# Giving the stores of the first layer's sums a later due time in a list-scheduled two-layer kernel

## The chip, the cores and the metric

One core of one Trainium2 chip runs the whole program. The metric is the device time of one execution in microseconds (us), taken as the median of several runs.

## The reference

The input is 8192 tokens of 192 values. A seven-tap convolution with softmax weights comes first, then two feed-forward layers with 2048 hidden units, each `x @ w_in`, an elementwise function, `@ w_out`:

```
x = attn_out.reshape(B * S, D)
h = np.maximum(x @ w_in, 0.0);  x = h * h @ w_out        # layer 0
h = x @ w_in;                   out = h * np.cos(h) @ w_out   # layer 1
```

All of it is float32. The kernel keeps that precision by writing each factor as a high part (`hi`, rounded) and a low part (`lo`, the rest), and by multiplying the parts on TensorE.

## The kernel before, in words

**Tiles.** The tokens are cut into 16 blocks of 512. For each layer m and block b there are 16 tiles f, one per 128 hidden units. So 512 tiles are counted through by t. Their order is `phases`: the first six blocks of layer 0, then layer 1 and layer 0 in turn, (1,0), (0,6), (1,1), (0,7) and so on, and the last six blocks of layer 1. For b from 5 on, block (0,b) ends at tile 96 + 32(b - 5) - 1, and 16 tiles of layer 1 follow it. A *site* below is such a stretch of 16 layer-1 tiles; there are eleven, for b = 5 to 15.

**What one tile does.** TensorE multiplies x by `w_in` into a PSUM bank `h` (line 618). For layer 1, `between` (from line 705) then scales and rounds on ACT (`rr`, line 721), subtracts on DVE (line 724), takes the absolute value and the sine on ACT (lines 726 and 727), multiplies by h on DVE (line 729, which is the last reader of the bank), and splits the product: `hi` is a copy (line 277 on ACT, line 279, a CAST, on DVE) and `lo` the difference (line 284, DVE or POOL). Six tiles later (`LAG`) TensorE multiplies `hi` and `lo` by `w_out` into the banks `acc` (line 642). There are four `h` banks, six `hi`, five `lo` and one set of `acc`.

**What follows a block.** Seven tiles after block (0,b) has ended, `take_x2(b)` adds up its sums and makes the second layer's input of them: four copies and additions out of `acc` (lines 277 and 740), then the *split*: a move between halves (`x2u`, line 277), its addition (`x2s`, line 748), two high parts on ACT (`x2t`, line 277) and two differences on DVE or POOL (`x2t` and `x2s`, line 284). Four stores on SP's queue (lines 770, 772, 775) write it to DRAM as `x2d`, from where `fetch` reads it as `X(1, b)` up to ten blocks later. `x2t` lies in the buffer `xt`, `x2s` in `sum`; there is one of each, and `take_out`, which does the same for layer 1, uses both next.

**Who sets the order.** The kernel lists all operations first and a scheduler (`Order.issue`) then puts them into engine queues. Each operation names the engines that it may run on, with a cost. A backward pass gives each operation a due time: TensorE's work is due at its place in time, a store at its `by`, and everything else early enough for its users. The forward pass takes, among the operations that could begin at once, the one with the earliest due time, and picks the engine on which it would end first. `clock(t)` is the planned time of tile t; a tile counts 2.155 us (`PACE`). Once built, each engine's queue is fixed and runs in order.

Of the kernel before, what the change touches and what calls it, by code (L numbers as in the profile page):

```python
# [25 lines left out]
LEAD = 6  # L26
# [34 lines left out]
class Order:  # L61
# [12 lines left out]
    def buf(self, pool, shape, dtype, tag, n, name):  # L74
        old = self.tags.setdefault(tag, [])
        b = Buf(
            lambda: pool.tile(shape, dtype, tag=tag, bufs=n, name=name),
            old[-n] if len(old) >= n else None, old[-1] if old else None,
        )
        old.append(b)  # L80
        return b
# [14 lines left out]
    def op(self, ways, fn, reads=(), writes=(), size=0, behind=None, by=1e9, over=(), since=0.0,  # L96
           alone=True, slack=0.0, ahead=0.0, drag=0.0):
        o = Op()
        o.ways, o.fn, o.size, o.drag = ways, fn, size, drag
        o.alone, o.slack, o.ahead = alone, slack, max(ahead, self.ahead)  # L100
        o.late = self.SENT + size / self.RATE + self.SEEN if size else 0.0
        o.behind, o.by, o.since = behind, by, max(since, self.since)
        o.older, o.deps, o.after, o.n = set(over), set(), set(behind or ()), len(self.ops)
        for write, accesses in ((False, reads), (True, writes)):
            for a in accesses:
                b, key = a if isinstance(a, tuple) else (a, None)
                for p, w, k in b.log:
                    if (w or write) and (k is None or key is None or k == key):
                        o.deps.add(p)
                if b.log:  # L110
                    o.after.add(b.log[0][0])
                elif b.before is not None:
                    o.after.add(b.before.log[0][0])
                if b.older is not None:
                    o.older.add(b.older)
                b.log.append((o, write, key))
        o.deps.discard(o)
        o.after.discard(o)
        self.ops.append(o)
        return o  # L120
# [57 lines left out]
def act(n, psum=False):  # L178
    return (0.05 if psum else 0.093) + n / 1200


def dve(n, fast=False, psum=False):
    return 0.147 + n / 960 if psum else 0.069 + n / (1600 if fast else 900)


def pool(n, scalar=False):
    return 0.1 + n * 0.0011 if scalar else 0.13 + n * 0.0023
# [3 lines left out]
def conv_moe_kernel(  # L191
# [40 lines left out]
    def sbuf(shape, dtype, tag, n, name):  # L232
        return buf(sb, shape, dtype, tag, n, name)
# [41 lines left out]
    def copy(e, out, in_):  # L275
        if e == "act":
            nc.scalar.activation(out, in_, AF.Copy)  # L277
        elif e == "dve":
            nc.vector.tensor_copy(out, in_)  # L279
        else:  # L280
            nc.gpsimd.tensor_scalar(out=out, in0=in_, scalar1=1.0, scalar2=0.0, op0=ALU.mult, op1=ALU.add)

    def sub(e, out, in0, in1):
        eng[e].tensor_tensor(out=out, in0=in0, in1=in1, op=ALU.subtract)  # L284
# [316 lines left out]
    def clock(t):  # L601
        return START + (early / NF * t if t < NF else early + PACE * (t - NF))

    first, final = {}, {}
# [134 lines left out]
    def sums(o, v0, w0, a1, u):  # L739
        add = lambda out, in0, in1: nc.vector.tensor_tensor(out=out, in0=in0, in1=in1, op=ALU.add)  # L740
        (low0, low1), (high0, high1) = o[0], o[-1]
        op({"act": act(N, True), "dve": dve(N, psum=True)}, lambda e: copy(e, v0(), high0.t), [high0], w0, alone=False)
        op({"act": act(N, True), "dve": dve(N, psum=True)}, lambda e: copy(e, a1.t, high1.t), [high1], [a1], alone=False)
        if len(o) > 1:
            op({"dve": dve(N, psum=True)}, lambda e: add(v0(), low0.t, v0()), [low0], w0, alone=False)
            op({"dve": dve(N, psum=True)}, lambda e: add(a1.t, low1.t, a1.t), [low1], [a1], alone=False)
        op({"act": act(N)}, lambda e: copy(e, u.t, a1.t[DB:P]), [a1], [u])
        op({"dve": dve(N), "pool": pool(N)}, lambda e: eng[e].tensor_tensor(
            out=a1.t[0:DB], in0=a1.t[0:DB], in1=u.t, op=ALU.add), [u], [a1])


    def take_x2(b):
        o = acc.pop((0, b))
        xt = sbuf([P, 2, BS * D], F32R, "xt", 1, f"x2t{b}")
        s = sbuf([P, N], F32, "sum", 1, f"x2s{b}")
        u = sbuf([DB, N], F32, "raw", 2, f"x2u{b}")
        there = src[b] = buf(dram, [2, D, N], F32, f"x2_{b}", 1, f"x2d{b}")
        v = lambda: xt.t[:, 1, 0:N].bitcast(F32)
        sums(o, v, [(xt, 1)], s, u)
        op({"act": act(N)}, lambda e: copy(e, xt.t[:, 0, 0:N], v()), [(xt, 1)], [(xt, 0)])  # L760
        op({"dve": dve(N), "pool": pool(N)}, lambda e: sub(e, xt.t[:, 1, 0:N], v(), xt.t[:, 0, 0:N].bitcast(F32)),
           [(xt, 0)], [(xt, 1)])
        rest = lambda: xt.t[0:DB, :, N:BS * D]
        wide = lambda: s.t[0:DB].rearrange("d (w n) -> d w n", w=2)
        op({"act": act(N)}, lambda e: copy(e, rest(), wide()), [s], [(xt, 2)])
        op({"dve": dve(N), "pool": pool(N)}, lambda e: sub(
            e, wide().bitcast(F32R), wide(), rest().bitcast(F32)), [(xt, 2)], [s])
        due = clock(final[0, b] + 12)
        for w in range(2):
            op({"sp": 0.5}, lambda e, w=w: nc.sync.dma_start(out=there.t[w, 0:P], in_=xt.t[:, w, 0:N].bitcast(F32)),  # L770
               [(xt, w)], [(there, w)], size=P * N * 4, by=due)
        op({"sp": 0.5}, lambda e: nc.sync.dma_start(
            out=there.t[0, P:D].rearrange("d (w n) -> d w n", w=2), in_=rest().bitcast(F32)), [(xt, 2)], [(there, 2)],
           size=DB * N * 4, by=due)
        op({"sp": 0.5}, lambda e: nc.sync.dma_start(out=there.t[1, P:D], in_=s.t[0:DB]),
           [s], [(there, 3)], size=DB * N * 4, by=due)
# [29 lines left out]
    for b in range(NB):  # L806
        when(final[0, b] + LAG + 1, take_x2, b)
        when(final[1, b] + LAG + 1, take_out, b)
        t = first[1, b]
        when(t - 8, x2, b)  # L810
        if b == 0:
            continue
        t = first[0, b]
        ago = lambda n: max(t - n, -1)
        far = NF + (4 if b < LEAD else 12)
        if b > 1:
            when(ago(far + 8), load_x, b)
        if b % CB == 0:
            c = b // CB
            if c == 1:  # L820
                when(ago(2 * NF - 6), load_g, c)
                when(ago(2 * NF - 9), soon, softmax, c, 0, CB)
            else:
                n = 14 + 9 * c
                when(n, early_exp, c, clock(n) + 15)
                when(max(ago(NF + far), n + 2), late_softmax, c)
        if b == 1:
            for i in range(BS):
                when(i, second_slot, i)
            when(4, second_x1)  # L830
            continue
        for n, f in ((far, attend), (far - 8, x1)):
            when(ago(n), *([soon] if b == CB else []), f, b)
# [69 lines left out]
```

## Time and profile before

| what | value |
|---|---|
| median of 3 runs | 1185.49 us (1185.39 to 1186.48) |
| the profiled execution | 1183.92 us |
| its span | 1182.1 us, 1.8 us less |
| busy: TensorE, ACT, DVE, POOL | 97%, 87%, 81%, 47% |

Busy shares are means over the whole span. TensorE's matmuls overlap, so idle time shows better in the row of its weight loads (PEld), which carry the waits.

### The profile page before, as it was taken

The numbers are of one execution on the slowest core, as the hardware profiler recorded it, in microseconds if no ns is written. First come the engines' busy times: TensorE is split into PE (matmuls) and PEld (weight loads), VectorE is DVE, ScalarE is ACT, GpSimd is POOL, SyncE is SP. The second block draws the span as 40 slices with busy tenths as digits, with TensorE's granted clock in tenths as the row PEclk, the third lists the DMA queues.
The fourth block names the chain that finished last, engine by engine and source line by source line (L and its number), as shares of the span: only waits on it lengthen the run. The fifth ranks groups of instructions, "written<-read, shape, count | busy, mean of one in ns | idle before, by whom it ended". The sixth has DMA issues, their size and how long they took to land.

```text
span 1182.1 us, 25854 instructions
## 1 busy us (share of the span) xinstructions
PE 1152.2 (97%) x9922; PEld 949.9 (80%) x9922; DVE 955.4 (81%) x1381; ACT 1023.7 (87%) x1892; POOL 550.8 (47%) x427
## 2 busy tenths in 40 slices
PE   7998999999999999999999999999999999999997
PEld 7776888887888888788887878888888888888885
DVE  7788788788897968879698887978757657888886
ACT  2897999999888897988889898888988889999996
POOL 0227557886363555525455452642603315544442
PEclk8999999999999999999999999999999999999999
DMA  8606877652443533344352344334143323223301
GB/s 207 185 18 158 242 183 201 164 141 70 94 115 68 123 81 66 91 95 122 64 118 62 62 115 81 78 71 95 35 87 82 68 55 81 40 42 68 68 9 20
DMA packets 126540, 112.96 MB, mean 96 GB/s; under 512 B 58192, under 2 KB 95568, under 8 KB 126416
## 3 DMA queue, kind: packets, MB, share of 16 engines
q1 hardware_dynamic: 124928, 110.78, 39.9%
q8 instruction: 78, 1.28, 0.5%
q10 hardware_dynamic: 1488, 0.52, 0.3%
q14 instruction: 46, 0.38, 0.1%
HBM read 78.70 MB, written 31.26 MB: 93 GB/s over the span
## 4 chain that ended last, share of the span: by engine, by line
PE 72%; ACT 11%; DVE 8%; DMA 4%; issue 2%; SPq 2%; POOL 1%; DVEq 0%; ACTq 0%
PE acc L642 37%; PE h L618 34%; ACT rr L721 2%; DVE lo L284 2%; ACT hi L277 2%; ACT rr L726 2%; DVE rr L729 2%; ACT rr L727 2%; DVE rr L724 2%; PE second L508 1%; SPq L501 1%; DVE hi L279 1%; ACT x2t L277 1%; DMA xc<-in_x_dram 1%; DMA X(0, 10)_136<-x1d 1%
## 5 line engine op out<-in xcount | busy, mean ns | idle before, releaser
L642 PE MATMUL acc<-hi,wo 64*128 64x512 f32 x3054 | 958.3, 387 | 1.4 <-DVE x2t L740 1.2
L642 PE MATMUL acc<-lo,wo 64*128 64x512 f32 x2036 | 774.8, 388 | 1.2 <-DVE lo L284 1.1
L642 PEld LDWEIGHTS acc<-hi,wo 64*128 64x128 f32 x3054 | 543.3, 184 | 59.6 <-DVE x2t L740 2.0
L284 POOL TENSOR_TENSOR lo<-rr,hi 128x512 fp32r<-128x512 f32 x187 | 244.9, 1313 | 410.2 <-DVE hi L279 163.2
L642 PEld LDWEIGHTS acc<-lo,wo 64*128 64x128 f32 x2036 | 374.7, 184 | 41.4 <-DVE lo L284 4.5
L284 DVE TENSOR_TENSOR lo<-rr,hi 128x512 fp32r<-128x512 f32 x229 | 205.3, 909 | 71.3 <-ACT hi L277 34.2
L456 POOL TENSOR_TENSOR pr<-xc,wgen_late 128x672 f32<-128x672 f32 x96 | 168.0, 1830 | 98.6 <-DVE at L471 79.1
L724 DVE SCALAR_TENSOR_TENSOR rr<-rr,h 128x512 f32<-128x512 int32 x256 | 173.8, 683 | 44.5 <-ACT rr L721 42.5
L711 ACT ACTIVATE rr<-h 128x512 f32<-128x512 f32 x256 | 152.5, 597 | 59.8 <-PE h L618 58.8
L729 DVE TENSOR_TENSOR rr<-h,rr 128x512 f32<-128x512 f32 x256 | 173.1, 685 | 29.5 <-ACT rr L727 28.2
L277 ACT ACTIVATE hi<-rr 128x512 fp32r<-128x512 f32 x288 | 178.8, 627 | 14.9 <-DVE rr L729 12.8
L726 ACT ACTIVATE rr<-rr 128x512 f32<-128x512 f32 x256 | 156.8, 626 | 27.2 <-DVE rr L724 27.1
L727 ACT ACTIVATE rr<-rr 128x512 f32<-128x512 f32 x256 | 157.9, 626 | 1.5
L721 ACT ACTIVATE rr<-h 128x512 int32<-128x512 f32 x256 | 149.8, 587 | 4.8 <-PE h L618 3.8
L715 ACT ACTIVATE rr<-rr 128x512 f32<-128x512 f32 x158 | 99.3, 629 | 2.1
L471 DVE TENSOR_REDUCE at<-pr 128x192 f32<-128x1344 f32 x56 | 86.2, 1545 | 0.4
L284 DVE TENSOR_TENSOR lo<-h,hi 128x512 fp32r<-128x512 f32 x96 | 64.1, 686 | 20.3 <-PE acc L642 15.1
L279 DVE CAST hi<-rr 128x512 fp32r<-128x512 f32 x128 | 64.6, 505 | 8.6 <-DVE rr L729 0.5
L277 ACT ACTIVATE hi<-h 128x512 fp32r<-128x512 f32 x96 | 57.9, 605 | 4.0 <-PE acc L642 2.7
L715 ACT ACTIVATE h<-rr 128x512 f32<-128x512 f32 x94 | 57.3, 612 | 1.6
L336 POOL TENSOR_TENSOR wilo_early<-wilo_early,wihi_early 128x384 uint32<-128x384 uint32 x16 | 17.0, 1070 | 59.2 <-DVE wilo_early L334 53.1
L618 PE MATMUL h<-X(0, 2)_110,wihi 64*128 64x512 f32 x96 | 28.6, 388 | 1.1 <-DMA X(0, 2)_110<-x1d 1.1
(237 smaller groups left out, 2910.3 us busy)
## 6 DMA issues: line engine op xcount, KB each, us to landing
xc<-in_x_dram SPq DMA_DIRECT2D x14, 960.0 KB, 6.0
x1d<-xt SPq DMA_DIRECT2D x104, 96.0 KB, 2.1
x2d<-x2t SPq DMA_DIRECT2D x32, 256.0 KB, 2.5
out_dram<-out SPq DMA_DIRECT2D x64, 64.0 KB, 2.0
rawo<-in_moe_w_out_dram SPq DMA_DIRECT2D x8, 384.0 KB, 3.6
x2d<-x2t SPq DMA_DIRECT2D x16, 128.0 KB, 2.6
x2d<-x2s SPq DMA_DIRECT2D x16, 128.0 KB, 2.4
out_dram<-ob SPq DMA_DIRECT2D x30, 64.0 KB, 1.9
```

The costliest lines, as they stand in the source:

```text
L277: nc.scalar.activation(out, in_, AF.Copy)
L284: eng[e].tensor_tensor(out=out, in0=in0, in1=in1, op=ALU.subtract)
L456: eng[e].tensor_tensor(out=t.rearrange("p k (h g) -> p k h g", h=H)[:, :, hs], in0=xc[b].t[:, i:i + K, :].rearrange("p k (h g) -> p k h g" ...
L618: return lambda: nc.tensor.matmul(h.t, lhsT=w[m].t[q, s, c], rhs=x[q, v, s], start=n == 0, stop=n == len(ops) - 1)
L642: nc.tensor.matmul(o[a].t, lhsT=wo[m].t[q, f, W[w]], rhs=p[v].t[q], start=f == 0 and n in (0, 3), stop=f == last_f and n in (2, 4))
L711: op({"act": act(N, True)}, lambda e: nc.scalar.activation(r.t, h.t, AF.Relu), [h], [r])
L715: nc.scalar.activation(g.t, r.t, AF.Square)
L721: op({"act": act(N, True)}, lambda e: nc.scalar.activation(k(), h.t, AF.Identity, scale=INV_2PI), [h], [r])
L724: op({"dve": dve(N, psum=True)}, lambda e: nc.vector.scalar_tensor_tensor(out=r.t, in0=k(), scalar=-TWO_PI, in1=h.t, op0=ALU.mult, op1=ALU ...
L726: op({"act": act(N)}, lambda e: nc.scalar.activation(r.t, r.t, AF.Abs), [], [r])
L727: op({"act": act(N)}, lambda e: nc.scalar.activation(r.t, r.t, AF.Sin, scale=-1.0, bias=math.pi / 2), [], [r], behind=exps if (b, f) == (0 ...
L729: op({"dve": dve(N, psum=True)}, lambda e: nc.vector.tensor_tensor(out=r.t, in0=h.t, in1=r.t, op=ALU.mult), [h], [r], alone=False)
```

## The change

The four stores of `take_x2` are due 18 tiles behind the end of their block instead of 12, for b >= 5 (`LEAD` is 6). That is 6 x 2.155 = 12.9 us later on the scheduler's clock, and by the backward pass the split in front of them is due later as well. No operation is added or taken out.

```diff
-        due = clock(final[0, b] + 12)
+        due = clock(final[0, b] + (18 if b >= LEAD - 1 else 12))
         for w in range(2):
             op({"sp": 0.5}, lambda e, w=w: nc.sync.dma_start(out=there.t[w, 0:P], in_=xt.t[:, w, 0:N].bitcast(F32)),
                [(xt, w)], [(there, w)], size=P * N * 4, by=due)
```

TensorE's queue stays the same row for row. The other queues are the same up to tile 96. From there, ACT has 18 rows more, DVE 11 and POOL 9 rows fewer (neighbouring equal rows are one), because the scheduler also chooses other engines: CASTs of `hi` on DVE go from 128 to 100, and ACT takes the 28. On SP only the order among the four stores of a block changes. The differences stand in the sites, and in the last 80 tiles.

ACT behind block (0,6), where `x2u6`, `x2t6` and `x2s6` belong to the split and the other names carry their tile. Before:

```order
L277 ACTIVATE x2u6_4881<-x2s6_4836 64x512
L721 ACTIVATE rr134_4900<-h134_4852 128x512
L277 ACTIVATE x2t6_4813<-x2t6_4813 128x512
L726 ACTIVATE rr133_4861<-rr133_4861 128x512
L726 ACTIVATE rr134_4900<-rr134_4900 128x512
L727 ACTIVATE rr133_4861<-rr133_4861 128x512
L277 ACTIVATE x2t6_4813<-x2s6_4836 64x2x256
L727 ACTIVATE rr134_4900<-rr134_4900 128x512
L721 ACTIVATE rr135_4944<-h135_4889 128x512
L277 ACTIVATE hi133_4950<-rr133_4861 128x512
```

and with the change:

```order
L277 ACTIVATE x2u6_4881<-x2s6_4836 64x512
L721 ACTIVATE rr134_4900<-h134_4852 128x512
L277 ACTIVATE hi132_4902<-rr132_4832 128x512
L726 ACTIVATE rr133_4861<-rr133_4861 128x512
L726 ACTIVATE rr134_4900<-rr134_4900 128x512
L727 ACTIVATE rr133_4861<-rr133_4861 128x512
L727 ACTIVATE rr134_4900<-rr134_4900 128x512
L721 ACTIVATE rr135_4935<-h135_4889 128x512
L277 ACTIVATE x2t6_4813<-x2t6_4813 128x512
L277 ACTIVATE hi133_4947<-rr133_4861 128x512
```

The first `x2t6` copy has moved behind six rows, the second has left this stretch, and `hi132` has come to ACT.

DVE at the same place. Before:

```order
L724 SCALAR_TENSOR_TENSOR rr134_4900<-rr134_4900,h134_4852 128x512
L279 CAST hi132_4925<-rr132_4832 128x512
L729 TENSOR_TENSOR rr133_4861<-h133_4822,rr133_4861 128x512
L729 TENSOR_TENSOR rr134_4900<-h134_4852,rr134_4900 128x512
L724 SCALAR_TENSOR_TENSOR rr135_4944<-rr135_4944,h135_4889 128x512
L284 TENSOR_TENSOR lo132_4967<-rr132_4832,hi132_4925 128x512
L284 TENSOR_TENSOR lo133_4979<-rr133_4861,hi133_4950 128x512
L729 TENSOR_TENSOR rr135_4944<-h135_4889,rr135_4944 128x512
```

and with the change:

```order
L724 SCALAR_TENSOR_TENSOR rr134_4900<-rr134_4900,h134_4852 128x512
L284 TENSOR_TENSOR lo132_4925<-rr132_4832,hi132_4902 128x512
L729 TENSOR_TENSOR rr133_4861<-h133_4822,rr133_4861 128x512
L729 TENSOR_TENSOR rr134_4900<-h134_4852,rr134_4900 128x512
L724 SCALAR_TENSOR_TENSOR rr135_4935<-rr135_4935,h135_4889 128x512
L724 SCALAR_TENSOR_TENSOR rr136_4963<-rr136_4963,h136_4917 128x512
L729 TENSOR_TENSOR rr135_4935<-h135_4889,rr135_4935 128x512
```

The CAST of `hi132` is gone, `lo132` stands in its place, and `lo133` has left the queue.

POOL at the same place. Before:

```order
L748 TENSOR_TENSOR x2s6_4836<-x2s6_4836,x2u6_4881 64x512
L284 TENSOR_TENSOR x2t6_4813<-x2t6_4813 128x512
L284 TENSOR_TENSOR x2s6_4836<-x2s6_4836,x2t6_4813 64x512
L284 TENSOR_TENSOR lo134_4992<-rr134_4900,hi134_4965 128x512
L284 TENSOR_TENSOR lo135_5012<-rr135_4944,hi135_5003 128x512
```

and with the change:

```order
L748 TENSOR_TENSOR x2s6_4836<-x2s6_4836,x2u6_4881 64x512
L284 TENSOR_TENSOR x2t6_4813<-x2t6_4813 128x512
L284 TENSOR_TENSOR lo133_4975<-rr133_4861,hi133_4947 128x512
L284 TENSOR_TENSOR lo134_4990<-rr134_4900,hi134_4977 128x512
L284 TENSOR_TENSOR lo135_5025<-rr135_4935,hi135_5008 128x512
L284 TENSOR_TENSOR lo136_5050<-rr136_4963,hi136_5039 128x512
L284 TENSOR_TENSOR lo137_5085<-rr137_4998,hi137_5068 128x512
L284 TENSOR_TENSOR x2s6_4836<-x2s6_4836,x2t6_4813 64x512
```

`lo133` has come to POOL, behind the `x2t6` difference, and the last difference of the split stands five rows later.

## Rows read from the trace of the kernel before

**Rows 1.** The page's busy times, and the granted TensorE clock in 40 slices.

```profile
PE 1152.2 (97%) x9922; PEld 949.9 (80%) x9922; DVE 955.4 (81%) x1381; ACT 1023.7 (87%) x1892; POOL 550.8 (47%) x427
PEclk8999999999999999999999999999999999999999
```

**Rows 2.** Busy time of PE by stretch: stretch, length, busy (matmuls), clock, DMA.

```profile
255.00:995.00 740.00, 734.80 (x6399) 1.00 0.37 83
1000.00:1160.00 160.00, 160.00 (x1414) 1.00 0.26 48
```

**Rows 3.** Waits of PEld from 255 to 1160 us: total us, times, longest.

```profile
PEld h L618 <- DVE rr L729: 11.5, 19, 1.6
PEld acc L642 <- DVE lo L284: 4.5, 8, 0.8
PEld acc L642 <- DVE x2t L740: 0.4, 1, 0.4
```

**Rows 4.** Timeline of PEld, site of block 6: start, duration, and idle before.

```profile
347.94 0.18 PEld L618 LDWEIGHTS h<-X(1, 1)_123,wilo 64*128 64x128 f32 x1 [0.41 <-DVE rr L729]
351.44 0.18 PEld L642 LDWEIGHTS acc<-lo,wo 64*128 64x128 f32 x1 [0.43 <-DVE lo L284]
355.11 0.18 PEld L618 LDWEIGHTS h<-X(1, 1)_123,wilo 64*128 64x128 f32 x1 [0.63 <-DVE rr L729]
```

**Rows 5.** Timeline of DVE, same site.

```profile
344.90 2.38 DVE L279 CAST hi<-rr 128x512 fp32r<-128x512 f32 x1
347.21 1.28 DVE L729 TENSOR_TENSOR rr<-h,rr 128x512 f32<-128x512 f32 x2
349.00 2.38 DVE L284 TENSOR_TENSOR lo<-rr,hi 128x512 fp32r<-128x512 f32 x2
...
354.37 0.68 DVE L729 TENSOR_TENSOR rr<-h,rr 128x512 f32<-128x512 f32 x1
```

**Rows 6.** Timeline of POOL, same site.

```profile
344.46 1.29 POOL L748 TENSOR_TENSOR x2s<-x2s,x2u 64x512 f32<-64x512 f32 x1
345.72 1.28 POOL L284 TENSOR_TENSOR x2t<-x2t 128x512 fp32r<-128x512 f32 x1
```

**Rows 7.** All CASTs of `hi` on DVE: duration ns min/median/max, first and last start.

```profile
L279 DVE CAST hi<-rr x128: 416/427/2392, 304.4 to 1169.5; 128x512 fp32r<-128x512 f32 x128
```

**Rows 8.** Timeline of ACT, site of block 6.

```profile
344.29 0.63 ACT L277 ACTIVATE x2t<-x2t 128x512 fp32r<-128x512 f32 x1
...
345.87 0.62 ACT L727 ACTIVATE rr<-rr 128x512 f32<-128x512 f32 x1
346.39 0.62 ACT L277 ACTIVATE x2t<-x2s 64x512 fp32r<-64x512 f32 x1
```

**Rows 9.** Timeline of PEld, sites of blocks 5, 7 and 13.

```profile
271.76 0.18 PEld L618 LDWEIGHTS h<-X(1, 0)_119,wilo 64*128 64x128 f32 x1 [0.30 <-DVE rr L729]
...
277.60 0.18 PEld L618 LDWEIGHTS h<-X(1, 0)_119,wilo 64*128 64x128 f32 x1 [1.63 <-DVE rr L729]
280.00 0.18 PEld L618 LDWEIGHTS h<-X(1, 0)_119,wilo 64*128 64x128 f32 x1 [0.48 <-DVE rr L729]
283.06 0.18 PEld L618 LDWEIGHTS h<-X(1, 0)_119,wilo 64*128 64x128 f32 x1 [0.70 <-DVE rr L729]
...
422.98 0.18 PEld L618 LDWEIGHTS h<-X(1, 2)_127,wilo 64*128 64x128 f32 x1 [0.90 <-DVE rr L729]
...
841.62 0.18 PEld L642 LDWEIGHTS acc<-lo,wo 64*128 64x128 f32 x1 [0.78 <-DVE lo L284]
```

**Rows 10.** Busy time of ACT by stretch, columns as in rows 2.

```profile
343.00:358.30 15.30, 14.66 (x29) 1.00 0.17 52
...
413.00:423.00 10.00, 9.95 (x20) 1.00 0.26 80
```

**Rows 11.** Tiles `x2d` and `out` between 330 and 400 us: durations ns, first and last start.

```profile
L501 SPq DMA_DIRECT2D X(1, 2)_127<-x2d x6: 600/604/623, 364.1 to 367.4; - x6
...
L277 ACT ACTIVATE out<-acc x1: 590/590/590, 374.2 to 374.2; 128x512 f32<-128x512 f32 x1
```

## The prediction

> **What bounds the kernel now.** I read the page's busy times first, and the reader is to see that TensorE is busy 97% of the span at a granted clock of 0.9 or more in all slices but the first; that is the upper of its two levels, 2.4 GHz [rows 1]. So the time can only shrink where TensorE stands still. How much that is shows in the count of matmuls by stretch [rows 2]. In the stretch from 1000 to 1160 us nothing holds it up, and it starts 1414 matmuls in 160 us, 8.84 per us. At that rate the 6399 matmuls of the stretch from 255 to 995 us need 724.1 us. They took 740, so **15.9 us** were lost.
>
> Who took them shows in the waits of the weight loads [rows 3]: 11.5 us for DVE's last product (line 729), which frees an `h` bank, 4.5 us for `lo`, and 0.4 us for the sums. That is 16.4 us in 28 waits, and nearly the 15.9 of the count; I scale waits by 15.9/16.4 = 0.97. All of them lie in the eleven sites. This is the whole stock from which the change can gain; before 255 us it moves nothing.
>
> **Why the waits are there.** At the site of block 6 TensorE waits three times, 0.41 + 0.43 + 0.63 = 1.47 us [rows 4]. The DVE timeline of the same 11 us shows the cause [rows 5]. The CAST of `hi132` begins at 344.90 and takes 2.38 us. The median CAST takes 0.43 [rows 7], so 1.95 us are lost. POOL runs two operations of the split end to end in that time, 344.46 to 345.75 and 345.72 to 347.00 [rows 6], and the CAST ends 0.28 us behind the second. Behind it in DVE's queue the product of tile 133 ends at 347.9 (first of the two at 347.21), while TensorE wants its bank at 347.5 (347.94 less 0.41). Then `lo132` and `lo133` take 2.38 us for two, `lo133` is late for 351.44, and the product of tile 136 (354.37) is late for 355.11. So one delay on DVE is handed down the queue, and the split starts it.
>
> The Trainium skill has a rule for such a pair ("SBUF — State Buffer", section "Who interferes with whom"): DVE in a two-port mode, or with two SBUF inputs, and POOL share a port pair, and the one that issues second blocks until the first has finished. The trace agrees that the CAST blocks, but it was passed over twice: behind the first operation alone it would have ended at about 346.2, and 1.1 us of the 1.95 would be missing. By the rule a bad meeting in the new order costs one POOL operation at most, 1.29 us; by the row it costs the run, and I price it at 1.95.
>
> **The change part by part.**
>
> *Removed from ahead of the critical work, even sites* (blocks 6, 8 and 10 to 15, which wait like block 6). ACT starts an operation every 0.52 us here (345.87, 346.39 in [rows 8]). The new row order puts `hi132` where the first `x2t6` copy was (344.29), which costs nothing more. With the second copy gone, the sine of tile 134 starts at 346.4 instead of 346.9, the scaling of 135 follows at 346.9, the moved `x2t6` copy at 347.4, and `hi133` at 347.9. DVE has no CAST. `lo132` may wait for POOL's addition to end at 345.75 and is done by 346.4. The sine of 133 ends at 346.49, so the product of 133 runs 346.5 to 347.2 instead of to 347.9, in time for 347.5. Rows of 0.52 us on ACT bring the sine of 135 to 350.0 and of 136 to 351.5; their products end at 351.3 and 352.9. The second ended at 355.05 before, and TensorE wants it at 353.6 (355.11 less the three waits). The 0.41 and the 0.63 go.
>
> *Added there.* `lo133` now stands on POOL behind the moved difference: copy ends 348.0, difference 349.3, `lo133` 350.6, with 1.28 us each [rows 6]. Before it ended at 349.00 + 2.38 = 351.38. Without its own wait and the one ahead of it TensorE wants it at 350.6 (351.44 less 0.43 and 0.41). So the 0.43 goes too, but barely. At block 13, which stands for the last three, the same wait was 0.78 [rows 9], 0.35 more. I leave 0.3 us at each of these three and 0.1 at the other five: 1.4 us. The ends are 0 and the largest wait for a `lo`, 0.8 [rows 3].
>
> *Odd sites* (blocks 7 and 9) have one wait of 0.90 [rows 9], for the product of tile 167 in the first. In the new order the scaling of 167 stands on ACT ahead of the split's rows, about three rows or 1.5 us earlier. Both waits go.
>
> *Block 5* waits 0.4 for the sums [rows 3] and then 0.30, 1.63, 0.48 and 0.70 us [rows 9]. Ahead of the first three of these five the order is unchanged; the third ends at 277.60. Behind it DVE had two differences of the split in front of the product of 102 and now one addition, and the product of 103 moves up further. The last two, 1.2 us, go; 2.3 stay.
>
> *Stores.* They leave some 12 us later. Behind them on SP's queue stands the load of `X(1, 2)`, issued at 364.1 [rows 11], with about 3 us to spare, and it feeds a block that starts 30 us later. `xt` and `sum` are wanted next at 374.2, by the first copy of `take_out`. Cost nothing, covered by those 3 and 10 us.
>
> *Engines changed.* 28 copies go from DVE (0.43 us) to ACT (0.52 us a row), about 2.5 per site. ACT is filled there to 96 and 99.5% [rows 10], yet the rows above already count them. *The last 80 tiles* are reordered without a wait to gain or a known one to lose: 0, with 0.9 us either way, one wait like that of an odd site.
>
> **Sum.** Waits 16.4 = 3.5 (block 5) + 1.8 (odd) + 11.1 (even). Gone: 1.2 + 1.8 + (11.1 - 1.4) = 12.7, times 0.97 = **12.3 us**. The profiled execution, 1183.92 us of which the span is 1182.1, would take 1171.6. The median of the runs is 1.57 us above that execution, and I predict against it: 1185.49 - 12.3 = **1173.2 us**. The bounds: all 15.9 gone and 0.9 us in the tail gives 1185.49 - 16.8 = 1168.7; with a `lo` late at all eight even sites by 0.78, 6.2 us instead of the 1.4 stay, the gain is (16.4 - 2.3 - 6.2) x 0.97 = 7.7, and it is 1177.8.
>
> **Rivals.**
>
> *ACT becomes the bound.* ACT has the fewest free microseconds in a site (0.64 of 15.3, 0.05 of 10 [rows 10]) and gets 2.5 rows more. If my row times slip by one row, 0.52 us, the products of the even sites lose their margin again: a wait like the 0.63 [rows 4] stays at eight sites and 0.9 at two, 6.8 x 0.97 = 6.6 us, and the gain is 12.3 - 6.6 = 5.7: **1179.8 us**. For it speaks the full engine; against it that the split's copies, two rows, left the critical stretch as well. The Trainium skill ("Perfetto Trace Analysis", section "Optimizing Scalar/DVE Operations") says that an operation with a DVE performance mode is faster there, and that handing it to ACT makes sense if DVE is saturated. The trace agrees on the first (0.43 against 0.62), and ACT is the fuller one, so by that rule this case decides. 14%.
>
> *POOL's run grows.* In the new order `x2t6`, `lo133` and `lo134` stand end to end, 3.8 us. A CAST or `lo` that meets them on DVE would lose up to 1.95 us again, and hand it down as before. At even sites no such row stands on DVE there; only a shift of several rows would bring one in. Then the waits stay as they are: **1185.5 us**, within 0.2%. So also if TensorE's waits come from something the due time does not touch. 6%.
>
> *Slower: the stores hold `xt` too long.* `take_out` needs `xt` and `sum` at 374.2, and the next block cannot add into `acc` before `take_out` has emptied it. The split's last difference now waits behind `lo137` on POOL and comes at about 360. If it slipped beyond 372, each us more would stall TensorE at eleven sites; 2 us give 22 - 12.3 = 9.7 us more, **1195 us**. For it: one buffer, later stores. Against it: 12 us of room. 4%.
>
> **How the numbers follow.** My forecast has 76%, the rivals 14, 6 and 4. About 0.2%, or 2.4 us, is what a measurement of this kernel can tell from no change. The forecast and the ACT rival are both faster by more: 0.9, less 2 for ends of theirs that come near nothing: 0.88. Same 0.07, slower 0.05. The range takes in the bounds of the forecast and the ACT rival at 1179.8, short of the lowest corner: 1169.5 to 1180.5.
>
> **What would show it.** After, the 28 waits of the weight loads come down to some ten and under 4.5 us, most of it in block 5 (0.4, 0.30 and 1.63 remain). At 340 to 360 us the three waits are gone, no CAST of 2.4 us stands on DVE, and `lo133` ends on POOL before TensorE asks. The stretch from 255 us on counts close to 8.84 matmuls per us. I am wrong if waits for line 729 turn up at even sites with ACT full, if `lo` waits grow beyond 0.3 us, or if waits appear where there were none, in the layer-0 blocks or the last 80 tiles.

## The result, and the profile after

The change makes the kernel faster: median 1172.18 us of 6 runs (1171.37 to 1175.54) against 1185.45 us of 6 (1183.22 to 1186.48), a ratio of 0.9895 with a 95% interval of 0.988 to 0.991. In a later series the same two kernels had a ratio of 0.9905 (0.9888 to 0.9921; 1173.50 us of 4 runs, 1184.51 us of 13). The forecast was 1173.2 us, so the prediction was right.

Two profiles of the changed kernel are read below. The first is of the run of 1175.54 us, the highest of the six; it holds one delay of some 2.5 us that the second, of a run of 1173.78 us in the later series, does not have (the last section shows it). Where a term is sized, the second is used.

The page of the first, busy times, granted clock and shares of the chain:

```profile
PE 1146.1 (98%) x9922; PEld 1020.8 (87%) x9922; DVE 952.3 (81%) x1370; ACT 1024.2 (87%) x1910; POOL 539.1 (46%) x420
PEclk9999999999999999999999999999999999999999
PE 90%; DVE 3%; ACT 3%; DMA 2%; POOL 1%; SPq 1%; issue 1%; DVEq 0%; ACTq 0%
```

DVE and POOL have less to do and ACT 0.5 us more than in [rows 1], but none of this is what the time is made of: the chain that ended last now runs to 90% over TensorE, where it was 72% before. The 87% of PEld is not an effect of the change; the second profile of the same kernel has 943.8 us, 81%.

How much TensorE still loses is counted as before, in the stretch from 255 to 995 us (second profile, columns as in [rows 2]; the clean stretch now ends at 1157 us, since the kernel's tail begins earlier):

```profile
255.00:995.00 740.00, 738.76 (x6504) 1.00 0.38 85
1000.00:1157.00 157.00, 157.00 (x1386) 1.00 0.23 44
```

The clean rate is unchanged, 1386/157 = 8.83 per us. At 8.84 the stretch could hold 6542 matmuls and holds 6504, so 4.3 us are lost there, where it was 15.9. The waits of the weight loads over 255 to 1160 us answer to [rows 3]. In the run of 1175.54 us they sum to 7.2 us, 2.54 of them the one delay; the run of 1173.78 us has:

```profile
PEld h L618 <- DVE rr L729: 2.3, 3, 1.7
PEld acc L642 <- POOL lo L284: 1.0, 3, 0.4
PEld acc L642 <- DVE x2t L740: 0.4, 1, 0.4
PEld acc L642 <- issue: 0.4, 1, 0.4
```

Eight waits and 4.1 us stand where there were 28 and 16.4. The last of them (0.4, issue) lies in the kernel's tail, and the kernel before has it too, behind the stretch that was counted, so 3.7 us belong to the sites: 2.7 to block 5 and 1.0 to the last three sites. Every wait for line 729 behind block 5 is gone, and seven of the eleven sites have no wait at all. The waits that are left in the second profile, by place (block 5, then block 13):

```profile
272.65 0.18 PEld L642 LDWEIGHTS acc<-hi,wo 64*128 64x128 f32 x1 [0.38 <-DVE x2t L740]
273.25 0.18 PEld L618 LDWEIGHTS h<-X(1, 0)_119,wilo 64*128 64x128 f32 x1 [0.30 <-DVE rr L729]
279.09 0.18 PEld L618 LDWEIGHTS h<-X(1, 0)_119,wilo 64*128 64x128 f32 x1 [1.66 <-DVE rr L729]
281.37 0.18 PEld L618 LDWEIGHTS h<-X(1, 0)_119,wilo 64*128 64x128 f32 x1 [0.37 <-DVE rr L729]
...
834.24 0.18 PEld L642 LDWEIGHTS acc<-lo,wo 64*128 64x128 f32 x1 [0.35 <-POOL lo L284]
```

The site of block 6 in the first profile shows the new order at work. DVE, where [rows 5] had the CAST of 2.38 us:

```profile
347.42 1.35 DVE L284 TENSOR_TENSOR lo<-rr,hi 128x512 fp32r<-128x512 f32 x1
348.99 1.29 DVE L729 TENSOR_TENSOR rr<-h,rr 128x512 f32<-128x512 f32 x2 [0.21 <-ACT rr L727]
```

and POOL, where [rows 6] had the run of two:

```profile
346.93 1.29 POOL L748 TENSOR_TENSOR x2s<-x2s,x2u 64x512 f32<-64x512 f32 x1
350.55 1.29 POOL L284 TENSOR_TENSOR x2t<-x2t 128x512 fp32r<-128x512 f32 x1 [2.33 <-ACT x2t L277]
351.80 2.56 POOL L284 TENSOR_TENSOR lo<-rr,hi 128x512 fp32r<-128x512 f32 x2
...
361.35 1.29 POOL L284 TENSOR_TENSOR x2s<-x2s,x2t 64x512 fp32r<-64x512 f32 x1 [0.81 <-ACT x2t L277]
```

POOL now idles 2.33 us behind the addition. `lo132` meets the addition alone and takes 1.35 us instead of some 0.7, and the product of tile 133 then waits 0.21 us for ACT, not for DVE's queue. No CAST anywhere is slow any more (the longest in [rows 7] took 2392 ns):

```profile
L279 DVE CAST hi<-rr x100: 416/427/434, 307.0 to 1156.4; 128x512 fp32r<-128x512 f32 x100
```

ACT at the sites of blocks 6 and 7 is as full as it was, or fuller [rows 10]:

```profile
344.50:359.80 15.30, 15.25 (x31) 1.00 0.09 35
413.00:423.00 10.00, 9.95 (x20) 1.00 0.01 2
```

### The profile page after: what moved, and what is told of

Same layout as the page of the kernel before. It is cut to its first block, busy times and chain, and to the rows that moved or that the text cites. A ratio compares the mean times of both kernels' runs of the same rounds, so it can differ in the third digit from the quotient of the medians.

```text
span 1173.7 us, 25854 instructions
## 1 busy us (share of the span) xinstructions
PE 1146.1 (98%) x9922; PEld 1020.8 (87%) x9922; DVE 952.3 (81%) x1370; ACT 1024.2 (87%) x1910; POOL 539.1 (46%) x420
## 4 chain that ended last, share of the span: by engine, by line
PE 90%; DVE 3%; ACT 3%; DMA 2%; POOL 1%; SPq 1%; issue 1%; DVEq 0%; ACTq 0%
PE acc L642 46%; PE h L618 42%; PE second L508 1%; DMA xc<-in_x_dram 1%; DVE lo L284 1%; ACT hi L277 1%; DMA X(0, 2)_110<-x1d 1%; ACT h L715 0%; DVE pr L456 0%; SPq L583 0%; DVE at L471 0%; POOL pr L456 0%; SPq L239 0%; ACT rr L711 0%; DVE wo_early L456 0%
## 5 line engine op out<-in xcount | busy, mean ns | idle before, releaser
L642 PE MATMUL acc<-hi,wo 64*128 64x512 f32 x3054 | 935.0, 388 | 1.5 <-DVE x2t L740 1.2
L642 PE MATMUL acc<-lo,wo 64*128 64x512 f32 x2036 | 758.4, 388 | 0.0
L642 PEld LDWEIGHTS acc<-hi,wo 64*128 64x128 f32 x3054 | 526.6, 185 | 39.3 <-DVE x2t L740 2.1
L284 POOL TENSOR_TENSOR lo<-rr,hi 128x512 fp32r<-128x512 f32 x175 | 226.6, 1298 | 381.7 <-DVE hi L279 144.9
L284 DVE TENSOR_TENSOR lo<-rr,hi 128x512 fp32r<-128x512 f32 x241 | 217.7, 914 | 63.5 <-ACT hi L277 34.3
L277 ACT ACTIVATE hi<-rr 128x512 fp32r<-128x512 f32 x316 | 197.7, 628 | 6.5 <-DVE rr L729 4.6
L284 DVE TENSOR_TENSOR lo<-h,hi 128x512 fp32r<-128x512 f32 x96 | 63.9, 684 | 21.0 <-PE acc L642 16.4
L279 DVE CAST hi<-rr 128x512 fp32r<-128x512 f32 x100 | 42.6, 426 | 6.9 <-ACT rr L715 1.8
L618 PE MATMUL h<-X(0, 2)_110,wihi 64*128 64x512 f32 x96 | 31.6, 410 | 1.4 <-DMA X(0, 2)_110<-x1d 1.4
```

The source lines that it names most:

```text
L618: return lambda: nc.tensor.matmul(h.t, lhsT=w[m].t[q, s, c], rhs=x[q, v, s], start=n == 0, stop=n == len(ops) - 1)
L642: nc.tensor.matmul(o[a].t, lhsT=wo[m].t[q, f, W[w]], rhs=p[v].t[q], start=f == 0 and n in (0, 3), stop=f == last_f and n in (2, 4))
```

## The experiments

### One site left as it was

```diff
-        due = clock(final[0, b] + (18 if b >= LEAD - 1 else 12))
+        due = clock(final[0, b] + (18 if b >= LEAD else 12))
```

> The later due time from block 6 on instead of from block 5 on. Theory of rank (the split's rows stand ahead of the tiles' rows and every site pays for its own split): the site of block 5 has its last two waits of the weight loads back, 0.48 and 0.70 us, and all other sites look as with the change; 1.2 us more than with the change. Rival (the change acts through the whole order behind block 5): waits at other sites differ too, and the time by more than 2 us.

1172.74 us, ratio to the kernel before 0.9907 (0.9888 to 0.9926). Block 5 has its five waits again (0.40, 0.30, 1.65, 0.47 and 0.67 us, as in [rows 3] and [rows 9]), and the other sites are as with the change. So what the change takes from block 5's waits comes from block 5's own split, and the other sites do not need it; what block 5 gains stays below 1 us.

### POOL out of the split

Due 12 as before, but the split's two differences may only run on DVE.

```diff
-        op({"dve": dve(N), "pool": pool(N)}, lambda e: sub(e, xt.t[:, 1, 0:N], v(), ...
+        op({"dve": dve(N)}, lambda e: sub(e, xt.t[:, 1, 0:N], v(), ...
...
-        op({"dve": dve(N), "pool": pool(N)}, lambda e: sub(
+        op({"dve": dve(N)}, lambda e: sub(
```

> Due time 12 as before, but the split's two differences may run on DVE alone, so that POOL never runs the split end to end. Theory of rank: the two rows now stand on DVE itself ahead of the products, 1.2 us; even sites still wait 1 us or more each, and the time is that of before within 4 us (1181 to 1189). Rival, the meeting of CAST and POOL's run is the whole cause: no CAST over 0.5 us in the sites, the even sites' 11.1 us of waits go, 1174 to 1176.

1199.69 us, ratio 1.0136 (1.0121 to 1.0151): slower. Two things are in this. The waits in the stretch from 255 us on did not fall:

```profile
PEld h L618 <- DVE rr L729: 15.4, 14, 1.8
```

At block 8 the CAST takes 1.13 us instead of 2.38, but the two differences now stand on DVE ahead of the critical rows, the second of them slow as well, and TensorE waits 1.41 us at 507.33 (DVE's timeline):

```profile
498.99 1.13 DVE L279 CAST hi<-rr 128x512 fp32r<-128x512 f32 x1
...
502.25 0.68 DVE L284 TENSOR_TENSOR x2t<-x2t 128x512 fp32r<-128x512 f32 x1
502.85 1.78 DVE L284 TENSOR_TENSOR x2s<-x2s,x2t 64x512 fp32r<-64x512 f32 x1
504.56 1.27 DVE L724 SCALAR_TENSOR_TENSOR rr<-rr,h 128x512 f32<-128x512 int32 x2
```

Second, the edit also reached blocks 0 to 4, which was not meant. Up to 255 us TensorE starts 1856 matmuls instead of 1981, some 14 us less work, with one wait of 9.81 us at 123.73. The cause of that wait was not followed. What the run does show: a faster CAST is not enough if the split stays early; it costs DVE then.

### The engines alone, and one copy alone

The first kernel keeps due 12 and sends the copies `hi` of the first twelve tiles of layer-1 blocks 0 to 10 to ACT; the second does so with the fifth tile of each alone, the one whose CAST is slow at blocks 6, 8, 10, 11 and 12.

```diff
+        near = m == 1 and b < NB - LEAD + 1 and f < 12
-        op({"act": act(N, True)} if own else {"act": act(N), "dve": dve(N, True)}, ...
+        op({"act": act(N, True)} if own else {"act": act(N)} if near else {"act": act(N), "dve": dve(N, True)}, ...
```

> Due time 12 as before, but the high parts of the first 12 tiles behind each first-layer block must be copied on ACT. Rival theory of the engines (the change gains because copies go from DVE to ACT): nearly the whole gain, 1173 to 1177. Theory of rank: ACT carries these copies and the split's copies ahead of the tiles' rows, products and low parts stay late; at least half of the waits remain, 1179 to 1190.

```diff
+        one = m == 1 and b < NB - LEAD + 1 and f == 4
-        op({"act": act(N, True)} if own else {"act": act(N), "dve": dve(N, True)}, ...
+        op({"act": act(N, True)} if own else {"act": act(N)} if one else {"act": act(N), "dve": dve(N, True)}, ...
```

> Due time 12 as before, one row changed per site: the high part of the site's fifth tile (tile 132 behind block 6) must be copied on ACT. If this one CAST in POOL's run starts the whole chain, even sites fall from 1.3 us to 0.5 or less, 1174 to 1178. If the number of copies on ACT or the rank of the split decides, even sites keep 0.9 us or more, 1180 to 1186.

The first took 1176.45 us, ratio 0.9941 (0.9926 to 0.9956), the second 1177.04 us, 0.9932 (0.9915 to 0.9948). In the second, no CAST is slow (median 427 ns, longest 436), and of the three waits at the site of block 6 one of 0.18 us is left; block 13 keeps 0.52, and the odd site of block 7 is not helped (timeline of PEld):

```profile
352.95 0.18 PEld L618 LDWEIGHTS h<-X(1, 1)_123,wilo 64*128 64x128 f32 x1 [0.18 <-DVE rr L729]
...
420.38 0.18 PEld L642 LDWEIGHTS acc<-lo,wo 64*128 64x128 f32 x1 [0.42 <-POOL lo L284]
422.85 0.18 PEld L618 LDWEIGHTS h<-X(1, 2)_127,wilo 64*128 64x128 f32 x1 [0.78 <-DVE rr L729]
...
837.94 0.18 PEld L618 LDWEIGHTS h<-X(1, 8)_151,wilo 64*128 64x128 f32 x1 [0.52 <-DVE rr L729]
```

The twelve copies of the first kernel do no more (0.45, 0.76 and 0.22 us at those places). So with this one copy on ACT most of the loss at an even site goes. It is not a test of that copy alone: in both kernels the scheduler also put the `x2t` difference on DVE, which breaks POOL's run, and `lo133` on POOL, so that DVE has no pair of `lo` of 2.38 us as in [rows 5] any more. The odd sites keep 0.76 and 1.2 us: copies on ACT do not clear them.

### The later split, with each copy on its old engine

Due 18, but in the layer-1 blocks 0 to 10 each `hi` runs on the engine that it had before the change.

```diff
+        CASTS = {1: (1, 2, 4, 8, 11, 12, 13, 14), ...
+        ways = {"act": act(N), "dve": dve(N, True)}
+        if m == 1 and b < NB - LEAD + 1:
+            ways = {"dve": dve(N, True)} if f in CASTS.get(b, ()) else {"act": act(N)}
-        op({"act": act(N, True)} if own else {"act": act(N), "dve": dve(N, True)}, ...
+        op({"act": act(N, True)} if own else ways, ...
```

> Due time 18 as with the change, but the high parts at the sites are forced onto the engines that they had before (the CASTs of even sites back on DVE). Theory of rank: the later split alone does it, since the CAST then meets one POOL operation and no run: waits at even sites under 0.3 us each, 1171 to 1175. Rival, the change of engine is needed: even sites keep 1 us or more each, 1181 to 1186. Between: the CAST still loses about 0.8 us to one operation and even sites keep 0.4 to 0.7, 1175 to 1179.

1174.27 us, ratio 0.9916 (0.9901 to 0.993). At even sites no wait is left, although the CAST of `hi132` is on DVE again and meets POOL. DVE:

```profile
343.50 1.13 DVE L279 CAST hi<-rr 128x512 fp32r<-128x512 f32 x1
345.12 1.29 DVE L729 TENSOR_TENSOR rr<-h,rr 128x512 f32<-128x512 f32 x2 [0.48 <-ACT rr L727]
```

and POOL:

```profile
343.06 1.29 POOL L753 TENSOR_TENSOR x2s<-x2s,x2u 64x512 f32<-64x512 f32 x1
344.78 1.30 POOL L284 TENSOR_TENSOR lo<-rr,hi 128x512 fp32r<-128x512 f32 x1 [0.43 <-DVE hi L279]
```

The CAST starts 0.44 us behind POOL's addition, as it did before (344.90 against 344.46). But now POOL idles 0.43 us behind the addition; the CAST ends 0.28 us behind it (344.63 against 344.35), 1.13 us long instead of 2.38, and the product behind it waits for ACT. So the second operation of the run makes the CAST as slow as it was, not the meeting alone. The order is not all that differs: the scheduler also moved `lo132` (the second POOL row, which waits for DVE's `hi`) and `lo133` to POOL, so here too the pair of `lo` has left DVE. At the odd site of block 7 two new waits stand, 0.29 and 1.15 us, since the forced CAST of tile 167 comes late there. For odd sites this run decides nothing.

### A later due time

```diff
-        due = clock(final[0, b] + (18 if b >= LEAD - 1 else 12))
+        due = clock(final[0, b] + (24 if b >= LEAD - 1 else 12))
```

> Due 24 tiles behind the block instead of 18. Theory of rank: the split is already behind the critical rows at 18, so the same waits as with the change within 1 us, 1170 to 1174. Rival, the stores hold the buffers too long: waits in front of the copies of the second layer's sums, 22 tiles behind the block, 1180 or more.

1172.87 us, ratio 0.9912 (0.9897 to 0.9927), the same as the change. Block 5 waits 2.7 us in all, as with 18, though 0.62 of it now for a `lo`; the other sites are as with the change. With 30 the rows of the program are those of 24. So 18 is on a flat part.

### What is left in block 5

Block 5's split meets an attention convolution on POOL and DVE. Here the one issued there (`attend(7)`) may not start before tile 114, once with due 18 and once with due 24; the third run repeats the second beside a repeat of the change.

```diff
+    def late_attend(b):
+        order.since = clock(114)
+        attend(b)
+        order.since = 0.0
...
+            if b == 7 and f is attend:
+                when(ago(n), late_attend, b)
+                continue
```

> The change, and the convolution of block 7 may not start before tile 114, so that its reductions (1.55 us each) leave DVE's queue at the site of block 5. If the rows ahead in DVE's queue make the wait of 1.63 us there, it goes and the site of block 5 falls from 3.0 us to about 1: 1169 to 1171. Rival: what the wait is for is set by ACT, the site keeps 2.5 us or more, 1171 to 1173, or the moved convolution makes new waits behind tile 112.

> Due 24 and the convolution of block 7 from tile 114 on, together. If both act on rows of their own: the site of block 5 below 1 us, the rest as with due 24; 1168.5 to 1171, no slower than either alone.

> Due 24 and the convolution of block 7 from tile 114 on, unaltered, beside the change on the same chip. If its 2 us less at the site of block 5 are real and nothing new takes them: 1 to 2 us below the change. Rival, the moved convolution meets low parts on DVE by chance behind tile 112: the same as the change, with waits there of up to 6 us in some executions.

> The change once more, unaltered, for a second profile. Its first profile had a wait of 2.54 us at the site of block 5 behind a low part on DVE that took 4.53 us; if that is chance, the site falls to 3.0 us here and the other sites stay as they were; median 1170 to 1174.

| kernel | us | ratio to before | 95% |
|---|---|---|---|
| later convolution, due 18 | 1175.74 | 0.9926 | 0.9911 to 0.9941 |
| later convolution, due 24 | 1171.69 | 0.9894 | 0.988 to 0.9909 |
| the same again | 1172.42 | 0.9894 | 0.9879 to 0.9909 |
| the change again | 1173.50 | 0.9905 | 0.9888 to 0.9921 |

Block 5 loses less, though not as little as the 1 us expected: 1.3 us with due 18 (0.72, 0.37 and 0.22), 1.4 with due 24 (0.80, 0.38 and 0.25). With due 18 this is paid back soon behind it. Twice a `lo` on DVE meets POOL's convolution, and TensorE waits 2.12 us at 296.70 and 2.15 us at 321.65. DVE at the first of the two:

```profile
291.91 4.13 DVE L284 TENSOR_TENSOR lo<-rr,hi 128x512 fp32r<-128x512 f32 x1
```

and POOL at the same time:

```profile
291.38 4.17 POOL L456 TENSOR_TENSOR pr<-xc,wgen_late 128x672 f32<-128x672 f32 x3
```

In both profiles with due 24 this is absent, but the site of block 6 has new waits (0.75 and 0.39 us, then 0.73 and 0.34). Both ratios with due 24 are 0.9894, where the change had 0.9895 and 0.9905; the intervals overlap almost wholly. No version was found that is clearly faster than the change.

### Stores that are really late

To see the slower rival, the four stores of a block may here not start before 32 tiles behind it.

```diff
         due = clock(final[0, b] + (18 if b >= LEAD - 1 else 12))
+        late = clock(final[0, b] + 32) if b >= LEAD - 1 else 0.0
-            ..., by=due)
+            ..., by=due, since=late)
```

> The change, and the four stores may not start before tile 32 behind the block on the scheduler's clock, 8 us later than the next user of the buffer would want it. The slower rival of the prediction: the copies of the second layer's sums come later by several us at eleven sites and TensorE waits for its banks, 2 us or more per site, 1190 or more. Theory that the buffers have room even then: 1174 or less.

1183.13 us of 8 runs, ratio 0.9985 (0.9971 to 0.9999): 9.6 us slower than the change in the same series, nearly all of its gain, though less than the 1190 us expected. The waits over 255 to 1160 us, the largest group:

```profile
PEld acc L642 <- ACT out L277: 8.4, 7, 3.3
```

Behind block 6 the last stores leave at 374.0 to 376.6 us, and the copy that wants their buffer starts at 382.0. With the change there is room (first profile, tile `x2d`, then `out`):

```profile
L772 SPq DMA_DIRECT2D x2d<-x2t x1: 560/560/560, 361.2 to 361.2; - x1
L775 SPq DMA_DIRECT2D x2d<-x2s x1: 477/477/477, 362.7 to 362.7; - x1
L501 SPq DMA_DIRECT2D X(1, 2)_127<-x2d x6: 602/604/618, 365.4 to 368.7; - x6
```

```profile
L277 ACT ACTIVATE out<-acc x1: 589/589/589, 375.6 to 375.6; 128x512 f32<-128x512 f32 x1
```

The last store is issued 12.9 us ahead of the copy, and 2.7 us ahead of the load behind it on SP's queue. The mechanism of the rival exists, but the change is far from it.

## Why the prediction was right

**The stock.** 15.9 us by count and 16.4 by waits, all in the eleven sites. Right. That a site's waits hang on its own split is shown for block 5: the run that leaves it as it was gives back its waits and no others.

**The cause at even sites.** "So one delay on DVE is handed down the queue, and the split starts it": that the early split costs the time is right, for its due time alone takes the waits away. The way there is not shown, and the kernel before speaks against the CAST as its start. It has the slow CAST at only five of the eight even sites (blocks 6, 8 and 10 to 12). At block 13 the CAST takes its usual time, the first product behind it waits for ACT, and the site still lost 0.78 + 0.62 = 1.40 us, against 1.47 at block 6 (DVE):

```profile
834.75 0.42 DVE L279 CAST hi<-rr 128x512 fp32r<-128x512 f32 x1
836.95 0.69 DVE L729 TENSOR_TENSOR rr<-h,rr 128x512 f32<-128x512 f32 x1 [1.78 <-ACT rr L727]
...
839.19 2.38 DVE L284 TENSOR_TENSOR lo<-rr,hi 128x512 fp32r<-128x512 f32 x2
```

What all eight sites have is the pair of `lo` in the last of these rows: 2.38 us, 1.1 more than two operations take that meet nothing, and each time beside a `lo` on POOL (at block 6, then at block 13):

```profile
349.23 1.60 POOL L284 TENSOR_TENSOR lo<-rr,hi 128x512 fp32r<-128x512 f32 x1 [0.79 <-ACT hi L277]
...
839.55 1.47 POOL L284 TENSOR_TENSOR lo<-rr,hi 128x512 fp32r<-128x512 f32 x1 [0.72 <-ACT hi L277]
```

So there are two delays on DVE at block 6, and the prediction took them for one. Every run that cleared most or all of the even sites (the change, the copies on ACT, the old engines) removed both, and taking POOL out of the split put two new rows on DVE instead. No run parts the two, and how much the slow CAST costs by itself stays open. ACT's order at block 13 is not quite that of block 6, so the two sites are no clean pair either.

The forecast of the new order did not need that answer, and it held row by row. The first profile runs 2.47 us later here (POOL's addition at 346.93 against 344.46). Less that, the product of tile 133 starts at 346.5 and `lo133` ends at about 350.6, both as forecast.

**Even sites, 1.4 us left.** 1.0 us is left: the 0.3 at each of the last three sites came as forecast, for `lo` on POOL behind the `x2t` difference (0.35 at block 13). The 0.1 at each of the other five came out as 0.

**Odd sites, 1.8 us.** All of it went, as forecast. Moving copies to ACT did not do it (0.76 and 1.2 us kept), so the later split did, directly or through what the scheduler placed with it; the run that was to part the two brought a new wait and leaves this open.

**Block 5, 1.2 us.** This is the term that was mis-sized. In the run of 1173.78 us its waits sum to 2.7 instead of 3.5, so 0.8 went. The last wait, 0.70, is gone, but the one before stays at 0.37 instead of 0.48. The step that failed is "one addition" in place of two differences, ahead of the product of tile 102. DVE before:

```profile
277.46 0.68 DVE L284 TENSOR_TENSOR x2t<-x2t 128x512 fp32r<-128x512 f32 x1
278.06 0.69 DVE L284 TENSOR_TENSOR lo<-rr,hi 128x512 fp32r<-128x512 f32 x1
278.67 0.68 DVE L284 TENSOR_TENSOR x2s<-x2s,x2t 64x512 fp32r<-64x512 f32 x1
279.27 0.68 DVE L729 TENSOR_TENSOR rr<-h,rr 128x512 f32<-128x512 f32 x1
```

and with the change (first profile; the second has the same lengths within 0.01):

```profile
280.62 1.17 DVE L748 TENSOR_TENSOR x2s<-x2s,x2u 64x512 f32<-64x512 f32 x1
281.72 0.67 DVE L724 SCALAR_TENSOR_TENSOR rr<-rr,h 128x512 f32<-128x512 int32 x1
282.32 0.68 DVE L729 TENSOR_TENSOR rr<-h,rr 128x512 f32<-128x512 f32 x1
```

and POOL beside it:

```profile
279.98 1.27 POOL L284 TENSOR_TENSOR x2t<-x2t 128x512 fp32r<-128x512 f32 x1
```

What stands ahead of the product took 1.81 us before (277.46 to 279.27) and takes 1.70 now (280.62 to 282.32); the 0.11 less is what the wait lost. Two things had been left out. The addition took 1.17 us, beside the difference that the scheduler had moved from DVE to POOL, the same kind of meeting that the prediction had found at the even sites. And a subtraction (line 724) now stands ahead of the product too, 0.6 us.

**The sum.** Gone by waits: 16.4 - 3.7 = 12.7, the forecast's 12.7, with 0.4 us too much in block 5 against 0.4 us too little at the even sites; that the two cancel is luck. Times 0.97 that is 12.3 us; the count gives 15.9 - 4.3 = 11.6, and the two series measured 13.3 and 11.0 us. Part of such a difference lies outside the sites: the second profile starts 1967 matmuls in its first 255 us and the profile before 1981, which is 1.6 us of work, though up to tile 96 the queues are the same.

**The rivals.** ACT as the bound did not come: ACT is busy 15.25 of 15.3 us at the site of block 6, and no wait for line 729 is left there. DVE's product there does wait for ACT (0.21 us), so ACT is now next in line, but inside TensorE's margin. The Trainium skill ("Perfetto Trace Analysis", section "Optimizing Scalar/DVE Operations") says that handing work from DVE to ACT may make sense if DVE is saturated. Here DVE was 81% and ACT 87% busy, and the 28 copies went to the fuller engine; 28 is the net number, 62 went to ACT and 34 came to DVE. The kernel with twelve copies a block on ACT gained 0.6% with the due time as it was: that ACT was the fuller engine did not stand in the way. POOL's longer run (`x2t`, `lo133`, `lo134`) slowed nothing on DVE at the site of block 6; but the 0.3 us at the last three sites are for a `lo` in that run, and in block 5 POOL's difference slowed DVE's addition. The stores held nothing.

## What to carry to other kernels

Size the stock first: count matmul starts in a clean stretch and in the lossy one; the difference and the sum of the waits should agree, as 15.9 and 16.4 did here, and a change that only takes waits away can gain no more than that. When an engine off the critical path runs two operations end to end, look at what the operation on DVE at that moment takes against its median; a late rank for side work with a far deadline can break the run at no cost. Before calling a slow row the cause, look in the same trace for a place that lacks it: here three sites without the slow CAST lost as much as the others. A due time moves more than the rows it names (here 96 copies changed engine), so test order and engines apart, and count an operation that comes beside POOL's at its slow length.

## What the hardware showed that was not expected

A DVE operation that meets a run of POOL operations is let in at different points of that run, with the same order of rows and the same offset. The run of 1175.54 us, DVE:

```profile
263.85 4.53 DVE L284 TENSOR_TENSOR lo<-rr,hi 128x512 fp32r<-128x512 f32 x1
```

and POOL:

```profile
262.30 5.62 POOL L456 TENSOR_TENSOR pr<-xc,wgen_late 128x672 f32<-128x672 f32 x4
```

The run of 1173.78 us of the same kernel, DVE:

```profile
264.93 1.76 DVE L284 TENSOR_TENSOR lo<-rr,hi 128x512 fp32r<-128x512 f32 x1
```

and POOL:

```profile
263.38 6.06 POOL L456 TENSOR_TENSOR pr<-xc,wgen_late 128x672 f32<-128x672 f32 x4
```

In both, `lo` starts 1.55 us behind the first of POOL's four products, and its median is 0.69 us. In one it is let in after 1.76 us, and POOL's run is 0.44 us longer; in the other it is passed over until the run ends, and TensorE waits 2.54 us for what stands behind it. The kernel before had 1.76 us at this place. The Trainium skill ("SBUF — State Buffer", section "Who interferes with whom") says that the one that issues second blocks until the first has finished. The 1.76 us fit one operation; the 4.53 us here, the 4.13 us with the later convolution and the 2.38 us of the CAST in [rows 5] do not, and the measurement decides: such a meeting can cost the whole run. What decides between the two was not found. The 2.54 us stand beside the 4.2 us by which the six runs of the changed kernel differ; the other five have no trace, so how much of their spread comes from such meetings stays open.
